# One accumulation for both heads of a pair, v in whole float32 beside zeros

## The chip, the core and the metric

The kernel runs on one core of a Trainium2 chip. The metric is the device time of one launch in microseconds: 1524.37 us, the median of three runs (1522.56, 1524.37 and 1529.31 us). TensorE is called PE below, its weight loads PEld; VectorE is DVE, ScalarE is ACT, GpSimd is POOL, SyncE is SP, which issues most DMAs.

## What is computed

Attention over 4 batches of 12 heads (448 positions, 64 values per head) with normalised q and k, followed by two mixers in float32, the first of rank 32 over the tokens and with 24 chunks of 128 channels, the second with a token mix and 12 chunks.

```python
q_n, k_n = rmsnorm(q, g_q), rmsnorm(k, g_k)
scores = np.matmul(q_n, k_n.transpose(0, 1, 3, 2)) / np.sqrt(64)
attn = softmax(scores)                       # with + 1e-9 below the line
x = np.matmul(attn, v)                       # (4, 12, 448, 64), then (4, 448, 768)
u = x + ((x.T @ U) @ V).T                    # first mixer
x = u + np.maximum(u @ w_ch1, 0) @ w_ch2     # w_ch1: 768 x 3072
h = np.maximum(x.T @ w_tok1, 0) @ w_tok2     # second mixer
u = x + h.T
out = u + np.maximum(u @ w_ch1b, 0) @ w_ch2b # 768 x 1536
```

The inputs of the mixers are float64, and the kernel turns their bits into float32 itself.

## The kernel before

Matmuls run in two forms: whole float32 operands (F32), or operands cut into a high and a low part of type float32r (F32R), whose products are added up. `split` (line 148) cuts: ACT writes the high part, POOL subtracts it for the low one.

The heads are taken in pairs, which share a tile of 128 partitions (2 x 64) of the result xT. The 12 pairs of batches 0 and 1 run alone: this is the lone stage. After it PE does the rank mix (`rank_mix`, line 588) of both batches, and the 12 pairs of batches 2 and 3 are woven into the channel mixer of the first two (`run`, line 1027). `attention` (line 513) sets the steps: at each step the softmax of a head two ahead, the weighting of the present one, the loads of a pair seven and five steps ahead. The program text is only the first order: a scheduler with a timeline model orders the instructions of each engine by readiness and by the buffers of the pools, so a change in one engine's load moves instructions on all of them. Engines then work in that order.

Per head the lone stage makes four score tiles sc (`softmax`, line 450): two F32R matmuls each, a maximum on DVE, the exponential on ACT, the scaling of p on POOL. `weigh` (line 471) then goes through four chunks of 112 keys: PE transposes four pieces of p into a PSUM tile pt, which is copied to SBUF as ph, and PE multiplies v by ph into the PSUM tile pv. The head of a pair with j = 0 is whole: v goes in as loaded (vr) and ph is a plain copy, by ACT or DVE in turn. The weights are 128 columns, of which the first 64 are the chunk's v, and only the first 64 rows of pv are used. The head with j = 1 is cut: v is split into vs (lines 403 to 410), ph is rounded to F32R by ACT, DVE makes the low part pl (line 502), and each chunk takes two F32R matmuls, of vs by ph and by pl. Its weights hold the high part of v beside the low one, so the two halves of pv are added at the end: ACT copies one to tmp (line 510), DVE adds it (line 511). For j = 0, DVE copies the half (line 507). In the woven stage both heads are cut.

In the lone stage the PSUM pools have 3 banks for sc ("s"), 1 for tt ("t"), and 4 ("p") that pt and pv share. In the trace one whole product of 448 columns shows as two MATMUL records, and one F32R product as one.

The mixer's weights are loaded in chunks (`load_w`, line 154): a DMA into w_raw, `to_f32` (line 118: ACT lines 130 and 135, DVE lines 131, 132 and 136, POOL line 139), then `split`. Their buffers hold two chunks of raw words and four of split weights.

Of the kernel before, what the change touches and what calls it, by code (L numbers as in the profile page):

```python
# [9 lines left out]
F32 = mybir.dt.float32  # L10
# [14 lines left out]
def attention_then_two_mixers(  # L25
# [30 lines left out]
    nc = tc.nc  # L56
    P = 128
    B, H, S, D = q.shape
# [298 lines left out]
    def fetch_heads(b, hp, names):  # L357

        h0 = 2 * hp
        res = []  # L360
        for nm in names:
            t = pools["at"].tile([CP, 2, NC4, D], F32, tag="vr" if nm == "v" else "qkr", bufs=AT[nm + "r"],
                        name=f"{nm}r")
            nc.sync.dma_start(t, dict(q=q, k=k, v=v)[nm][b, h0:h0 + 2].rearrange(
                "h (p c) d -> p h c d", c=NC4))
            res.append(t)
        return res

    def load_pair(b, hp, turn, qk):
        first = turn == 0  # L370
        mul = nc.vector.tensor_mul if turn in (0, 2, 3) else nc.gpsimd.tensor_mul
        qr, kr, vr = qk + fetch_heads(b, hp, "v")
# [30 lines left out]
    def split_v(vr, whole):  # L403
        vs = pools["at"].tile([CP, 2, NC4, 2, D], F32R, tag="vs", bufs=AT["vs"], name="vs")
        js = [j for j in range(2) if j not in whole]
        if js:
            js = slice(js[0], js[-1] + 1)
            split(vr[:, js], vs[:, js, :, 0], vs[:, js, :, 1])
        flat = vr.rearrange("p h c d -> p (h c d)")
        return [flat[:, j * NC4 * D:] if j in whole else vs[:, j] for j in range(2)]  # L410
# [59 lines left out]

    def weigh(pr, vj, j, dst, whole):

        pv = psum("v", [P, S], "pv")

        def product(kc, ph, pl):
            if whole:
                mm(pv, vj[:, kc * D:kc * D + P], ph, kc == 0, kc == NC4 - 1)
                return
# [27 lines left out]
        if whole:  # L506
            nc.vector.tensor_copy(dst[j * D:(j + 1) * D], pv[:D])
            return
# [4 lines left out]
    def attention(pairs, seam):  # L513
# [13 lines left out]
        for t in range(-8, n):  # L527
# [5 lines left out]
            if t >= 0:  # L533
                if t % 2 == 0:
                    dst = pairs[t // 2][3]()
                steps.append(weigh(
                    probs.pop(t), values[t // 2][t % 2], t % 2, dst, t % 2 in pairs[t // 2][2]))
# [19 lines left out]
            if 0 <= h < n:  # L557
                loaded[h // 2] = load_pair(
                    *pairs[h // 2][:2], h // 2, fetched.pop(h // 2))
# [499 lines left out]
    with ExitStack() as stack:  # L1059
# [3 lines left out]
        open_pools(inner, (("pp", 1, 0), ("s", 3, 1), ("t", 1, 1), ("p", 4, 1)))  # L1063
        pools["v"] = pools["p"]

        def new_xo():
# [3 lines left out]
            [(b, hp, (0,), lambda xT=xT, hp=hp: xT[:, hp], lambda dst: None)  # L1070
             for b, xT in zip((b0, b1), xs) for hp in range(NP)]
            + [(b, hp, (), new_xo,
                lambda dst, b=b, hp=hp: nc.sync.dma_start(xd[b][hp], dst))
               for b in (b2, b3) for hp in range(NP)], 2 * H)
# [114 lines left out]
```

## Time and profile before

| | us |
|---|---|
| median of three runs | 1524.37 |
| span of the profiled execution, first to last instruction | 1530.0 |
| lone stage, to the last addition into xT | 194.7 |
| rank mix of both batches and first products of the mixer | 194.7 to 232 |
| PE / DVE / POOL / ACT busy over the span | 1440.5 / 1177.0 / 908.4 / 745.0 |
| PE weight loads busy | 1274.2 |

The page gives no time for the profiled execution besides its span, which is 5.6 us over the median of the timed runs. Busy times are the union of an engine's instructions; matmuls overlap in the records, so that the cost of one on PE is read from the distance between the starts of neighbours and not from its length.

### The profile page before, as it was taken

Reading aid. Unit: us, or ns where it says so; the run is one execution under the profiler, and the core shown is the slowest. Engines: PE = TensorE matmul, PEld = TensorE weight load, DVE = VectorE, ACT = ScalarE, POOL = GpSimd, SP = SyncE. Lnnn points to the kernel's source line nnn. Section 1 sums busy time; section 2 is a strip of 40 time slices with the busy share of each in tenths; the row PEclk is TensorE's granted clock in tenths of the full one; section 3 lists DMA queues with packets and bytes.
Section 4 is the critical chain, followed back from the end, with each engine's and each line's share of the span. In section 5 each row is a group of like instructions: output and inputs, shape, how many; then the busy total and the mean of one; then the engine's idle time right before and its main releaser. Section 6 shows DMA issues by size and latency. Waiting matters only on the chain.

```text
span 1530.0 us, 22086 instructions
## 1 busy us (share of the span) xinstructions
PE 1440.5 (94%) x7396; PEld 1274.2 (83%) x7396; DVE 1177.0 (77%) x1805; ACT 745.0 (49%) x1508; POOL 908.4 (59%) x943
## 2 busy tenths in 40 slices
PE   4899988999899999999999999999999999999998
PEld 3666767888788889888888998898999998988997
DVE  7898888977787788676757776477888988577786
ACT  4687765765565665444535343335343431334431
POOL 5889947777666565455655454037787855206842
PEclk9999989999999999999999999999999999999999
DMA  6676656866666565765637664354545363423433
GB/s 174 156 168 158 151 169 208 273 201 199 223 207 202 165 207 189 248 228 189 213 125 239 227 232 143 115 194 130 181 125 185 125 192 122 130 92 109 137 117 108
DMA packets 144385, 266.06 MB, mean 174 GB/s; under 512 B 12832, under 2 KB 104448, under 8 KB 144160
## 3 DMA queue, kind: packets, MB, share of 16 engines
q1 hardware_dynamic: 143952, 264.65, 55.4%
q8 instruction: 59, 0.97, 0.3%
q14 instruction: 54, 0.44, 0.1%
q10 hardware_dynamic: 320, 0.00, 0.0%
HBM read 149.72 MB, written 79.10 MB: 150 GB/s over the span
## 4 chain that ended last, share of the span: by engine, by line
PE 50%; DVE 9%; DMA 4%; ACT 3%; POOL 3%; issue 2%; SPq 0%; DVEq 0%; POOLq 0%; ACTq 0%
PE ps_x L79 23%; PE ps_p L79 10%; PE ps_g L79 10%; PE ps_t L79 2%; PE ps_u L79 2%; DVE w_bits L136 1%; DVE w_bits L131 1%; DVE w_bits L132 1%; PE pv L79 1%; ACT w_bits L130 1%; POOL w L150 1%; DMA w_raw<-in_moe_w_ch_dram 1%; PE pt L487 1%; DMA c_a<-w_bits 1%; DMA qs<-both 1%
## 5 line engine op out<-in xcount | busy, mean ns | idle before, releaser
L79 PE MATMUL ps_x<-gs,w 128*128 128x448 f32 x1440 | 326.2, 373 | 7.6 <-DVE gs L656 2.9
L79 PE MATMUL ps_g<-u,w 128*128 128x448 f32 x1440 | 313.3, 371 | 6.5 <-DVE u L583 2.6
L79 PEld LDWEIGHTS ps_x<-gs,w 128*128 128x128 f32 x1440 | 268.6, 191 | 33.7 <-DVE gs L656 5.8
L79 PEld LDWEIGHTS ps_g<-u,w 128*128 128x128 f32 x1440 | 270.5, 190 | 30.3 <-DVE u L583 3.5
L79 PE MATMUL ps_x<-gs,w_b 128*128 128x448 f32 x1026 | 228.7, 368 | 6.5 <-DVE xT L851 2.0
L139 POOL TENSOR_TENSOR w_bits<-w_bits,w_round 128x768 uint32<-128x768 uint32 (+3 forms) x80 | 145.0, 1812 | 119.9 <-DVE w_bits L136 68.3
L79 PEld LDWEIGHTS ps_x<-gs,w_b 128*128 128x128 f32 x1026 | 192.7, 189 | 24.7 <-DVE xT L851 3.4
L150 POOL TENSOR_TENSOR w<-w_bits,w 128x768 fp32r<-128x768 f32 (+3 forms) x82 | 148.1, 1815 | 83.0 <-ACT w L149 78.6
L686 DVE TENSOR_TENSOR xT<-ps_x,xT 128x448 f32<-128x448 f32 x216 | 132.3, 618 | 44.5 <-PE ps_x L79 42.1
L150 POOL TENSOR_TENSOR w_b<-w_f,w_b 128x384 fp32r<-128x384 f32 x104 | 118.8, 1155 | 61.5 <-ACT w_b L149 61.1
L79 PE MATMUL sc<-ks,qs 128*112 128x448 f32 x384 | 124.6, 410 | 20.1 <-ACT p L461 16.9
L468 POOL TENSOR_SCALAR p<-p,sm 112x448 f32<-112x448 f32 x192 | 131.2, 696 | 19.4 <-DVE sm L465 16.1
L300 POOL TENSOR_TENSOR w_f<-w_f 128x384 f32<-128x384 f32 x26 | 36.4, 1401 | 178.7 <-DVE pu L779 73.5
L461 ACT ACTIVATE p<-sc,nm 112x448 f32<-112x448 f32 x192 | 121.4, 635 | 39.1 <-DVE nm L459 37.6
L459 DVE TENSOR_REDUCE nm<-sc 112x1 f32<-112x448 f32 x192 | 116.1, 614 | 11.8 <-PE sc L79 11.3
L487 PEld LDWEIGHTS pt<-ident,p 112*112 112x112 f32 x768 | 89.6, 135 | 34.3 <-issue 12.7
L487 PE MATMUL pt<-ident,p 112*112 112x112 f32 x768 | 110.6, 262 | 4.8 <-DVE pl L502 3.7
L498 ACT ACTIVATE ph<-pt 112x448 fp32r<-112x448 f32 (+1 forms) x168 | 88.2, 544 | 38.9 <-PE pt L487 38.0
L131 DVE TENSOR_SCALAR w_bits<-w_bits 128x768 f32<-128x768 f32 (+3 forms) x80 | 66.7, 834 | 50.0 <-ACT w_bits L130 50.0
L135 ACT ACTIVATE w_round<-w_raw 128x768 uint32<-128x768 uint32 (+3 forms) x80 | 69.8, 873 | 66.9 <-POOL w_bits L139 62.4
L502 DVE TENSOR_TENSOR pl<-pt,ph 112x448 fp32r<-112x448 f32 x144 | 86.9, 615 | 19.2 <-ACT ph L498 18.7
L130 ACT ACTIVATE w_bits<-w_raw 128x768 f32<-128x768 f32 (+3 forms) x80 | 70.0, 875 | 58.7 <-POOL w L150 31.4
(141 smaller groups left out, 2724.1 us busy)
## 6 DMA issues: line engine op xcount, KB each, us to landing
w_raw<-in_moe_w_ch_dram SPq DMA_DIRECT2D x72, 768.0 KB, 5.2
w_b<-h_a SPq DMA_DIRECT2D x65, 384.0 KB, 4.2
h_a<-w SPq DMA_DIRECT2D x56, 384.0 KB, 2.7
ks<-both SPq DMA_DIRECT2D x92, 224.0 KB, 3.7
c_a<-w_bits SPq DMA_DIRECT2D x40, 384.0 KB, 4.8
w_f<-c_a SPq DMA_DIRECT2D x40, 384.0 KB, 3.1
h_b<-w SPq DMA_DIRECT2D x32, 384.0 KB, 2.5
w_b<-h_b SPq DMA_DIRECT2D x29, 384.0 KB, 3.9
```

The source lines that it names most:

```text
L79: nc.tensor.matmul(o, lhsT=l, rhs=r, start=start, stop=stop)
L130: nc.scalar.activation(f(w), f(high), AF.Abs)
L131: nc.vector.tensor_scalar_max(f(w), f(w), TINY)
L139: nc.gpsimd.tensor_tensor(w, w, r, op=ALU.add)
L150: nc.gpsimd.tensor_sub(lo, w, f(hi))
L459: nc.vector.tensor_reduce(nm, sc, axis=AX.X, op=ALU.max, negate=True)
L461: nc.scalar.activation(p, sc, AF.Exp, bias=nm, accum_out=sm[:, c % 2:c % 2 + 1])
L468: nc.gpsimd.tensor_scalar(x, x, sm[:, i:i + 1], 1.0, op0=ALU.mult, op1=ALU.mult)
L487: nc.tensor.transpose(pt[:, c * CP:(c + 1) * CP], pr[c][:, kc * CP:(kc + 1) * CP], ident[:CP, :CP],)
L498: nc.scalar.activation(ph, pt, AF.Copy)
L502: nc.vector.tensor_sub(pl, pt, f(ph))
L686: nc.vector.tensor_add(xT[:, dc], px, xT[:, dc])
```

## The change

In the lone stage both heads of a pair are whole. v is loaded into one of four fixed buffers of 112 x 4 x 3 x 64, whose middle third is set to zero once by POOL; the two heads go, by one DMA each, to the thirds beside it. The weights of j = 0 are then (v, 0) and those of j = 1 are (0, v), each 128 columns, and all eight products of the pair accumulate in one PSUM tile, with the first matmul of j = 0 as its start and the last of j = 1 as its end. One DVE copy of 128 x 448 takes it to xT. ph is a plain copy for both heads, two by ACT and two by DVE. The split of v, pl, tmp and the addition are gone from this stage. The four shared PSUM banks become three for pt ("p") and one for pv ("v"). The woven stage computes as before.

```diff
-    def fetch_heads(b, hp, names):
+    def fetch_heads(b, hp, names, padded=None):
...
         for nm in names:
-            t = pools["at"].tile([CP, 2, NC4, D], F32, tag="vr" if nm == "v" else "qkr", bufs=AT[nm + "r"],
-                        name=f"{nm}r")
-            nc.sync.dma_start(t, dict(q=q, k=k, v=v)[nm][b, h0:h0 + 2].rearrange(
-                "h (p c) d -> p h c d", c=NC4))
-            res.append(t)
+            src = dict(q=q, k=k, v=v)[nm][b, h0:h0 + 2].rearrange("h (p c) d -> p h c d", c=NC4)
+            if nm == "v" and padded:
+                w = padded.pop(0)
+                padded.append(w)
+                for j in range(2):
+                    nc.sync.dma_start(w[:, :, 2 * j], src[:, j])
+            else:
+                w = pools["at"].tile([CP, 2, NC4, D], F32, tag="vr" if nm == "v" else "qkr",
+                                     bufs=AT[nm + "r"], name=f"{nm}r")
+                nc.sync.dma_start(w, src)
+            res.append(w)
         return res
-    def load_pair(b, hp, turn, qk):
+    def load_pair(b, hp, turn, qk, padded):
         first = turn == 0
         mul = nc.vector.tensor_mul if turn in (0, 2, 3) else nc.gpsimd.tensor_mul
-        qr, kr, vr = qk + fetch_heads(b, hp, "v")
+        qr, kr, vr = qk + fetch_heads(b, hp, "v", padded)
...
     def split_v(vr, whole):
+        if whole:
+            return [vr[:, :, j:j + 2].rearrange("p c h d -> p c (h d)") for j in range(2)]
         vs = pools["at"].tile([CP, 2, NC4, 2, D], F32R, tag="vs", bufs=AT["vs"], name="vs")
-        js = [j for j in range(2) if j not in whole]
-        if js:
-            js = slice(js[0], js[-1] + 1)
-            split(vr[:, js], vs[:, js, :, 0], vs[:, js, :, 1])
-        flat = vr.rearrange("p h c d -> p (h c d)")
-        return [flat[:, j * NC4 * D:] if j in whole else vs[:, j] for j in range(2)]
+        split(vr, vs[:, :, :, 0], vs[:, :, :, 1])
+        return [vs[:, j] for j in range(2)]
...
+    joint = []
+
     def weigh(pr, vj, j, dst, whole):
-        pv = psum("v", [P, S], "pv")
+        pv = joint.pop() if whole and j else psum("v", [P, S], "pv")
+        if whole and not j:
+            joint.append(pv)
...
             if whole:
-                mm(pv, vj[:, kc * D:kc * D + P], ph, kc == 0, kc == NC4 - 1)
+                mm(pv, vj[:, kc], ph, j == 0 and kc == 0, j == 1 and kc == NC4 - 1)
                 return
...
         if whole:
-            nc.vector.tensor_copy(dst[j * D:(j + 1) * D], pv[:D])
+            if j:
+                nc.vector.tensor_copy(dst, pv)
             return
...
-    def attention(pairs, seam):
+    def attention(pairs, seam, padded):
...
                 steps.append(weigh(
-                    probs.pop(t), values[t // 2][t % 2], t % 2, dst, t % 2 in pairs[t // 2][2]))
+                    probs.pop(t), values[t // 2][t % 2], t % 2, dst, pairs[t // 2][2]))
             for _ in zip_longest(*steps):
...
                 loaded[h // 2] = load_pair(
-                    *pairs[h // 2][:2], h // 2, fetched.pop(h // 2))
+                    *pairs[h // 2][:2], h // 2, fetched.pop(h // 2), h < seam and padded)
                 if h == 0:
...
         AT.update(p=12, ph=4, pl=4)
-        open_pools(inner, (("pp", 1, 0), ("s", 3, 1), ("t", 1, 1), ("p", 4, 1)))
-        pools["v"] = pools["p"]
+        open_pools(inner, (("pp", 1, 0), ("s", 3, 1), ("t", 1, 1), ("p", 3, 1), ("v", 1, 1)))
+        padded = []
+        for i in range(4):
+            padded.append(pools["pp"].tile([CP, NC4, 3, D], F32, tag=f"vp{i}", name="vr"))
+            nc.gpsimd.memset(padded[i][:, :, 1], 0.0)
...
         att = attention(
-            [(b, hp, (0,), lambda xT=xT, hp=hp: xT[:, hp], lambda dst: None)
+            [(b, hp, True, lambda xT=xT, hp=hp: xT[:, hp], lambda dst: None)
              for b, xT in zip((b0, b1), xs) for hp in range(NP)]
-            + [(b, hp, (), new_xo,
+            + [(b, hp, False, new_xo,
                 lambda dst, b=b, hp=hp: nc.sync.dma_start(xd[b][hp], dst))
-               for b in (b2, b3) for hp in range(NP)], 2 * H)
+               for b in (b2, b3) for hp in range(NP)], 2 * H, padded)
...
```

The scheduler's order of the whole lone stage and of the woven stage is another with the change; behind the last attention step the orders of all engines agree. Two places matter below. The first is PE in the middle of the lone stage. Before, the products of one pair's cut head (vs) and of the next pair's whole head (vr) alternate, in two PSUM tiles:

```order
L79 MATMUL pv<-pl,vs 128x448
L79 MATMUL pv<-ph,vs 128x448
L487 MATMUL pt<-ident,p 112x112 x4
L79 MATMUL sc<-ks,qs 112x448 x2
L79 MATMUL pv<-ph,vr 128x448
L79 MATMUL sc<-ks,qs 112x448 x2
L79 MATMUL pv<-pl,vs 128x448
L487 MATMUL pt<-ident,p 112x112 x4
L418 MATMUL tt<-ident,qn 128x112 x4
L79 MATMUL pv<-ph,vr 128x448
L487 MATMUL pt<-ident,p 112x112 x4
```

With the change, the end of the fourth pair and the start of the fifth; all eight products of a pair go into the one tile, and the second vr row below is the fourth pair's last:

```order
L79 MATMUL pv<-ph,vr 128x448
L495 MATMUL pt<-ident,p 112x112 x4
L79 MATMUL sc<-ks,qs 112x448 x6
L79 MATMUL pv<-ph,vr 128x448
L495 MATMUL pt<-ident,p 112x112 x8
L422 MATMUL tt<-ident,qn 128x112 x4
L495 MATMUL pt<-ident,p 112x112 x2
L79 MATMUL sc<-ks,qs 112x448 x2
L495 MATMUL pt<-ident,p 112x112
L79 MATMUL sc<-ks,qs 112x448 x2
L495 MATMUL pt<-ident,p 112x112
L79 MATMUL pv<-ph,vr 128x448 x3
```

The pairs no longer overlap in their products: 12 transposes pt, 4 transposes tt and 4 score matmuls stand between the last product of one pair and the first of the next. Over the eleven seams of the stage there stand 8 to 16 pt there, with up to 8 sc and at most 4 tt.

The second place is DVE, where it first meets a chunk of the mixer's weights (w_bits of 128 x 768). Before, that is behind the last addition into xT, among the rank mix's work (xs):

```order
L502 TENSOR_TENSOR pl<-pt,ph 112x448
L379 TENSOR_REDUCE ms<-sq 112x8
L511 TENSOR_TENSOR xT<-pv,tmp 64x448
L577 TENSOR_TENSOR xs<-pt_x,xs 112x384 x2
L131 TENSOR_SCALAR w_bits<-w_bits 128x768
L132 TENSOR_SCALAR w_bits<-w_bits 128x768
L136 SCALAR_TENSOR_TENSOR w_bits<-w_raw,w_bits 128x768
L577 TENSOR_TENSOR xs<-pt_x,xs 112x384 x2
```

With the change, that is in the middle of the lone stage, around the fifth of its twelve copies into xT:

```order
L504 COPY ph<-pt 112x448
L463 TENSOR_REDUCE nm<-sc 112x1 x3
L131 TENSOR_SCALAR w_bits<-w_bits 128x768
L516 COPY xT<-pv 128x448
L385 TENSOR_REDUCE ms<-sq 112x8
L504 COPY ph<-pt 112x448
L132 TENSOR_SCALAR w_bits<-w_bits 128x768
L463 TENSOR_REDUCE nm<-sc 112x1 x2
L136 SCALAR_TENSOR_TENSOR w_bits<-w_raw,w_bits 128x768
L469 RECIPROCAL sm<-sm 112x2
```

By the end of the lone stage DVE and POOL have converted none of these chunks before, and four with the change; ACT and POOL have also split two of the four there.

## Rows read from the trace of the kernel before

**Rows 1.** Windows: us, busy (instructions) of PE, PEld, DVE, ACT, POOL, clock, DMA, GB/s.

```profile
0.00:45.00 45.00, 24.62 (x111) 17.56 (x112) 33.50 (x64) 21.03 (x58) 25.94 (x55) 0.92 0.70 177
45.00:175.00 130.00, 119.11 (x682) 88.34 (x681) 114.28 (x238) 100.02 (x274) 116.64 (x213) 0.99 0.64 158
175.00:194.70 19.70, 16.63 (x96) 11.59 (x94) 14.90 (x29) 13.03 (x32) 16.87 (x34) 0.97 0.64 169
194.70:232.00 37.30, 31.95 (x147) 25.67 (x148) 32.18 (x55) 24.61 (x45) 15.22 (x11) 0.88 0.51 172
232.00:620.00 388.00, 368.00 (x1978) 326.64 (x1977) 311.64 (x526) 236.40 (x487) 258.28 (x284) 0.98 0.66 206
```

**Rows 2.** Groups of PE, 45 to 175 us: count, busy, mean ns, idle before.

```profile
L79 PE MATMUL sc<-ks,qs 128*112 128x448 f32 x152 | 49.6, 416 | 6.5 <-ACT p L461 5.0 <-DMA ks<-both 1.5
...
L487 PE MATMUL pt<-ident,p 112*112 112x112 f32 x300 | 40.4, 259 | 0.5 <-DVE sm L465 0.3 <-ACT ph L498 0.2
L79 PE MATMUL pv<-ph,vr 112*128 112x448 f32 x75 | 35.5, 554 | 0.0
...
L79 PE MATMUL pv<-ph,vs 112*128 112x448 f32 x37 | 16.8, 453 | 0.4 <-ACT ph L498 0.3
...
L418 PE MATMUL tt<-ident,kn 112*128 112x112 f32 x40 | 5.9, 272 | 0.0
```

**Rows 3.** Timeline of PE: start, length over the merged instructions, both us.

```profile
106.75 0.37 PE L79 MATMUL pv<-pl,vs 112*128 112x448 f32 x1
106.95 0.55 PE L487 MATMUL pt<-ident,p 112*112 112x112 f32 x4
...
107.74 0.92 PE L79 MATMUL pv<-ph,vr 112*128 112x448 f32 x2
108.50 0.55 PE L487 MATMUL pt<-ident,p 112*112 112x112 f32 x4
108.88 0.93 PE L79 MATMUL pv<-ph,vr 112*128 112x448 f32 x2
```

**Rows 4.** Waits of PE, 45 to 175 us: total us, times, longest.

```profile
PE sc L79 <- ACT p L461: 5.0, 8, 2.3
```

**Rows 5.** Groups of DVE, ACT, POOL for v, 45 to 175 us.

```profile
L502 DVE TENSOR_TENSOR pl<-pt,ph 112x448 fp32r<-112x448 f32 x38 | 22.8, 612 | 2.2 <-ACT ph L498 2.1
...
L498 ACT ACTIVATE ph<-pt 112x448 fp32r<-112x448 f32 x37 | 19.4, 548 | 5.3 <-PE pt L487 5.1
...
L496 DVE COPY ph<-pt 112x448 f32<-112x448 f32 x19 | 11.7, 615 | 0.1
...
L150 POOL TENSOR_TENSOR vs<-vr,vs 112x256 fp32r<-112x256 f32 x9 | 6.6, 728 | 0.1
...
L511 DVE TENSOR_TENSOR xT<-pv,tmp 64x448 f32<-64x448 f32 x9 | 5.6, 618 | 0.7 <-ACT tmp L510 0.4
...
L510 ACT ACTIVATE tmp<-pv 64x448 f32<-64x448 f32 x10 | 5.4, 541 | 0.2
...
L149 ACT ACTIVATE vs<-vr 112x256 fp32r<-112x256 f32 x10 | 4.2, 416 | 4.9 <-PE pv L79 4.9
```

**Rows 6.** Timeline around one copy of a weighted sum.

```profile
178.20 0.92 PE L79 MATMUL pv<-ph,vr 112*128 112x448 f32 x2
...
180.47 0.61 DVE L507 COPY xT<-pv 64x448 f32<-64x448 f32 x1
```

**Rows 7.** Groups of DVE for the weights, 192 to 232 us.

```profile
L136 DVE SCALAR_TENSOR_TENSOR w_bits<-w_raw,w_bits 128x768 uint32<-128x768 uint32 x4 | 4.4, 1092 | 0.0
...
L131 DVE TENSOR_SCALAR w_bits<-w_bits 128x768 f32<-128x768 f32 x4 | 2.2, 560 | 0.7 <-ACT w_bits L130 0.6
L132 DVE TENSOR_SCALAR w_bits<-w_bits 128x768 uint32<-128x768 uint32 x4 | 2.2, 553 | 0.0
```

**Rows 8.** Groups of POOL for the weights, 192 to 232 us.

```profile
L150 POOL TENSOR_TENSOR w<-w_bits,w 128x768 fp32r<-128x768 f32 x4 | 7.5, 1884 | 3.9 <-ACT w L149 3.9
L139 POOL TENSOR_TENSOR w_bits<-w_bits,w_round 128x768 uint32<-128x768 uint32 x4 | 7.5, 1865 | 18.2 <-DVE w_bits L136 18.2
```

## Prediction

> **What bounds the kernel now.** The first view is the windows by stage. The reader is to see that four engines are dense in the lone stage: from 45 to 175 us PE is busy 119.1 of 130 us, POOL 116.6, DVE 114.3, ACT 100.0 [rows 1]. No engine alone is full, and each could be the one that sets the pace. PE's busy share is flattering, because matmuls overlap in the records, so I count what PE has to do from the distances between starts. In the timeline of PE an F32R product is followed after 0.20 us (106.75 to 106.95), four transposes after 0.38 us (108.50 to 108.88, 0.095 each), and a whole float32 product, which has two records, after 0.76 us (107.74 to 108.50) [rows 3]. The groups give the counts: 152 sc at 0.20 are 30.4 us, 300 pt at 0.095 are 28.5, 75 records of vr, so 37.5 products at 0.76, are 28.5, the 37 products with ph and vs and as many with pl are 15 together at 0.20, and 80 tt (40 of k shown, 40 of q) are 7.6 [rows 2]. The sum is 110.0 us of 130, 85%. 37.5 products are 9.4 pairs: 13.8 us per pair, 11.7 of them work of PE. The waits say what the other 20 us are: small gaps, the largest group 5.0 us of sc for the exponential on ACT [rows 4]. So the lone stage is a chain through four nearly full engines, with PE at 85%.
>
> The next stretch is another case. From 194.7 to 232 us PE is busy 31.9 of 37.3 us at a mean clock of 0.88, and DVE 32.2, while POOL has only 15.2 [rows 1]. There the rank mix needs DVE for short steps, and DVE converts four chunks of weights between them [rows 7]; POOL waits 18.2 us for these conversions [rows 8].
>
> **What the change costs on PE.** Per pair four chunks of the cut head go from two F32R products (0.40) to one whole product (0.76): 4 x 0.36 = 1.44 us more, 17.3 us over 12 pairs. I take the same 0.76 for weights with zeros, since the columns streamed are the same 448. In the 9.4 pairs of the middle stretch it is 13.5 us: 123.5 us of work.
>
> **What it takes off the others.** Per pair DVE loses four pl (0.612) and the addition (0.618), gains two copies ph (0.615), and has one copy into xT as before, of 128 rows instead of 64 (both ends of the row count I price at 0.61): 1.84 us less, 22 us in all. ACT loses two ph (0.548), tmp (0.541) and the high part of v (0.416): 2.05 us, 25 in all. POOL loses the low part of v, 0.73 us, 9 in all [rows 5, 6]. None of this is a gain by itself. What it buys is that PE waits less, at most the 20 us that PE has free.
>
> **What the lone stage makes of it.** If PE were never idle, 123.5 us would be left of the 130; if PE stayed idle as long as now, 143.5. Between these I need PE's share in a stretch where the other engines are less full. The nearest is the woven stage: 1978 matmuls in 388 us [rows 1], of which 480 are transposes by the code (24 heads by 16 and 12 pairs by 8); 480 x 0.095 + 1498 x 0.20 = 345 us is 89%, an estimate, since some have fewer columns. There DVE is at 80% and POOL at 67%; with the change DVE would be at about 75% here (114.3 less 9.4 x 1.84), POOL still over 80%. I take 91%: 123.5 / 0.91 = 135.7, +5.7 us. Bounds: 96% gives -1.4, the idle time of now +13.5. The other 2.6 pairs stand at the ends of the stage, where PE is less dense (24.6 of 45 us, 16.6 of 19.7 [rows 1]); of their 3.7 us on PE I count half, 1.8, and the last head loses pl and tmp from its chain (0.61 + 0.54): +0.6 together. The lone stage: +6.3 us, between -2 and +17.
>
> **The conversions that move.** The order puts the conversion of four weight chunks into the lone stage, where DVE now has room. In the stretch from 192 to 232 us four of them cost DVE 4 x (0.560 + 0.553 + 1.092) = 8.8 us [rows 7]. They lie on the engine that is 86% busy there and that PE waits for, so I count most of it, -7 us; the bounds are -8.8 (all of it) and 0 (PE's lower clock and the chain of the rank mix bind alone). In the lone stage they are paid in DVE's free time, and POOL takes four additions of 1.87 and two subtractions of 1.88 us more, 11 us against the 9 that it loses [rows 5, 8]: POOL stays as full as it was. This is why I don't go above 91% for PE.
>
> **At nothing.** Four memsets of 112 x 256: a POOL subtraction of that size takes 0.73 us [rows 5], so at most 2.9 us at the start, where POOL is idle 19 of 45 us [rows 1]; if this cover failed, +2.9. Twelve more v loads on SP: they are issued five steps ahead into four fixed buffers, and a buffer comes free three heads before. The woven stage has another order but the same instructions, 0 with 3 us either way.
>
> **The one PSUM tile for pv.** The first product of a pair now waits until DVE has copied the pair before. In the trace a whole pair of records began at 178.20 and ended at 179.12, the copy began at 180.47 and ended at 181.08: 2.0 us behind the product [rows 6]. What hides it is the work of PE between two pairs in the new order. At the costs of [rows 3] the eleven seams have 1.1 to 3.1 us, mostly 2.3, so only the last one shows, 0.8 us, which lies within my bounds. On this the Trainium skill (Perfetto Trace Analysis, Matmuls) speaks against the change: independent groups of matmuls should rotate through different PSUM banks, so that the evacuation of one overlaps the next. By that rule the seam is a rival, below.
>
> **Sum.** +6.3 - 7 = -0.7 us on the profiled span of 1530.0, which is 5.6 us over the median; on the median of 1524.4 it gives 1523.7.
>
> **Rivals.** First, PE was not the limit, and fills up once DVE and ACT have room: 96% in the lone stage (-1.4) and all of the conversions (-8.8), 1514.2. For it: the largest wait of PE [rows 4] is for ACT, which is relieved. Against it: POOL is not relieved, and PE's free share would have to fall from 15 to 4%. The Trainium skill (Perfetto Trace Analysis, Identifying the Most-Contended Engine) would favour this one: it takes the busy share of the weight loads, not of the matmuls, as the measure of how full TensorE is. That share is 88.3 of 130 us, 68%, and both forms of product load two sets of weights, so by it nothing becomes tighter. But the starts in the timeline differ, 0.76 against 0.40 us, and this the weight loads don't show.
>
> Second, the gaps of PE are the latency of the chain and not the load of other engines, so that they stay: +17.3 - 7 = +10.3, 1534.7. For it: the gaps are many and short, and the products now come in blocks. Against it: DVE alone gets back 1.84 of 13.8 us per pair.
>
> Third, slower by the one PSUM tile: the copy stands in DVE's queue behind maxima, sums and a conversion of weights, and PE, which works in order, holds everything behind the first product, the scores too, so that DVE gets its next work late. It decides from 2.3 us between the last product and the end of the copy. At 3.0 us the eleven seams lose 7 us, at 3.5 us 12; with the latter 6.3 + 12 - 7 = +11, 1535.7. Against it: 2.0 us in the trace, with a fuller DVE.
>
> **How the numbers follow.** The forecast gets 0.50, the first rival 0.25, the second 0.15, the third 0.10. 1512 to 1536 leaves out the ends where both terms fall on one side; the forecast's own range is 1517 to 1531. Half a percent, 7.6 us, is about what can be told from no change. Faster by more: most of the first rival and a little of the forecast, 0.25; slower: most of the last two, 0.22; within: 0.53.
>
> **What would show it.** Starts of whole products 0.76 us apart from what follows them; a lone stage that ends near 201 us, with some 14.3 us per pair in the middle and PE waiting for POOL and ACT in small pieces; the first products of the mixer with hardly a conversion of DVE before them, and the point that was reached at 232 us reached some 30 us after the end of the lone stage. A wait of PE for L516, the copy into xT, of more than 0.5 us per pair would be the third rival. I am wrong if the lone stage ends before 194 or after 206 us, or if the stretch behind it takes as long as before.

## The result, and the profile after

The changed kernel takes 1547.18 us against 1526.84 us of the kernel before on the same chip, a ratio of 1.0149 (95% interval 1.0109 to 1.0189): slower by some 20 us, where 1523.7 us and a range of 1512 to 1536 were forecast. Timed again beside the experiments it was 1543.92 against 1521.32 us, 1.0138 (1.0108 to 1.0169).

The windows of the changed kernel (columns as in [rows 1]) are cut at the end of its lone stage (212.7 us), at the first product ps_x of the channel mixer (243.3) and at the 145th (369.6):

```profile
45.00:175.00 130.00, 118.54 (x600) 79.17 (x600) 97.81 (x197) 83.21 (x226) 112.68 (x187) 0.97 0.76 188
175.00:212.70 37.70, 35.42 (x186) 23.50 (x184) 23.95 (x49) 19.41 (x50) 30.37 (x61) 1.00 0.45 112
212.70:243.30 30.60, 25.48 (x135) 21.56 (x136) 21.65 (x43) 14.18 (x31) 1.84 (x1) 0.96 0.04 14
243.30:369.60 126.30, 112.12 (x590) 97.59 (x588) 99.81 (x170) 76.41 (x161) 94.16 (x107) 0.96 0.71 213
```

The same cuts of the kernel before, at 194.7, 229.3 and 345.5 us, and the stretch behind them up to its 289th ps_x:

```profile
194.70:229.30 34.60, 29.32 (x137) 23.68 (x137) 29.48 (x51) 21.91 (x41) 12.71 (x9) 0.87 0.47 155
229.30:345.50 116.20, 108.16 (x569) 92.80 (x568) 98.72 (x164) 73.42 (x154) 86.20 (x99) 0.99 0.74 228
345.50:449.40 103.90, 95.43 (x509) 85.59 (x507) 81.71 (x136) 60.78 (x127) 71.70 (x82) 0.95 0.64 196
```

The lone stage is 18.0 us longer, the stretch to the first ps_x 4.0 us shorter, and the next 144 products take 10.1 us more. In the windows from 45 to 175 us DVE fell from 114.3 to 97.8 of 130 us and ACT from 100.0 to 83.2, while POOL went from 116.6 to 112.7 and the DMA share rose from 0.64 to 0.76. The last row belongs to the profiled execution of before alone: it spent 103.9 us there at a clock of 0.95, and a variant with the same number of products in this stretch takes 96.8 us at 1.00 (below). So traces are compared up to 345 us only, and totals by the timed runs.

The groups of PE in the changed kernel, 45 to 175 us, answer to [rows 2]:

```profile
L79 PE MATMUL pv<-ph,vr 112*128 112x448 f32 x130 | 59.5, 557 | 0.7 <-ACT ph L506 0.7
L79 PE MATMUL sc<-ks,qs 128*112 128x448 f32 x139 | 44.0, 412 | 6.2 <-ACT p L465 5.9
L495 PE MATMUL pt<-ident,p 112*112 112x112 f32 x263 | 39.8, 267 | 4.6 <-ACT ph L506 2.8 <-POOL p L472 1.1 <-DVE ph L504 0.7
L422 PE MATMUL tt<-ident,kn 112*128 112x112 f32 x36 | 5.5, 274 | 0.0
L422 PE MATMUL tt<-ident,qn 112*128 112x112 f32 x32 | 4.4, 259 | 0.0
```

By the distances of [rows 3] this is 65 x 0.76 + 139 x 0.20 + 263 x 0.095 + 68 x 0.095 = 108.7 us of work in 130, 84%, where it was 85%. 65 products are 8.1 pairs, 16.0 us each. The distances themselves hold; in the timeline of PE a whole product starts, and what follows it 0.75 us later:

```profile
94.37 0.91 PE L79 MATMUL pv<-ph,vr 112*128 112x448 f32 x2
95.12 0.93 PE L495 MATMUL pt<-ident,p 112*112 112x112 f32 x8
```

The waits of PE from 45 to 212.7 us (total, times, longest) are small pieces as in [rows 4], and the copy out of the joint tile is waited for once:

```profile
PE sc L79 <- ACT p L465: 5.9, 6, 2.4
PE pt L495 <- ACT ph L506: 2.8, 2, 1.8
PE pv L79 <- DVE xT L516: 1.3, 1, 1.3
```

### The profile page after: what moved, and what is told of

The parts are those of the page before. It is cut to its first block, busy times and chain, and to the rows that moved or that the text cites. A ratio compares the mean times of both kernels' runs of the same rounds, so it can differ in the third digit from the quotient of the medians.

```text
span 1542.2 us, 22000 instructions
## 1 busy us (share of the span) xinstructions
PE 1450.7 (94%) x7396; PEld 1268.2 (82%) x7396; DVE 1157.3 (75%) x1769; ACT 723.1 (47%) x1460; POOL 905.7 (59%) x935
## 4 chain that ended last, share of the span: by engine, by line
PE 44%; DVE 6%; DMA 3%; POOL 3%; ACT 2%; issue 2%; SPq 0%; POOLq 0%; ACTq 0%; DVEq 0%
PE ps_x L79 21%; PE ps_p L79 10%; PE ps_g L79 8%; PE ps_u L79 2%; PE ps_t L79 2%; POOL w L150 1%; DVE w_bits L131 1%; POOL w_bits L139 1%; DMA c_a<-w_bits 1%; ACT w_bits L130 1%; DVE w_bits L136 1%; DVE w_bits L132 1%; DMA w_raw<-in_moe_w_ch_dram 1%; ACT w L149 1%; PE pt_x L579 1%
## 5 line engine op out<-in xcount | busy, mean ns | idle before, releaser
L472 POOL TENSOR_SCALAR p<-p,sm 112x448 f32<-112x448 f32 x192 | 139.7, 740 | 23.3 <-DVE sm L469 21.0
L495 PE MATMUL pt<-ident,p 112*112 112x112 f32 x768 | 113.9, 264 | 6.5 <-POOL p L472 2.8
L131 DVE TENSOR_SCALAR w_bits<-w_bits 128x768 f32<-128x768 f32 (+3 forms) x80 | 70.2, 877 | 59.3 <-ACT w_bits L130 59.2
L79 PE MATMUL ps_p<-t,w_b 128*128 128x448 f32 x432 | 95.1, 366 | 0.1
L799 ACT ACTIVATE pu<-pu 128x448 f32<-128x448 f32 x56 | 32.4, 579 | 132.5 <-DVE pu L788 132.1
```

The source lines that it names most:

```text
L79: nc.tensor.matmul(o, lhsT=l, rhs=r, start=start, stop=stop)
L131: nc.vector.tensor_scalar_max(f(w), f(w), TINY)
L472: nc.gpsimd.tensor_scalar(x, x, sm[:, i:i + 1], 1.0, op0=ALU.mult, op1=ALU.mult)
L495: nc.tensor.transpose(pt[:, c * CP:(c + 1) * CP], pr[c][:, kc * CP:(kc + 1) * CP], ident[:CP, :CP],)
```

## Experiments on the two parts

Ends of the lone stage are the ends of the last write into xT in the timeline of DVE; before it is 194.7 us. Ratios are to the kernel before, with 95% intervals.

**hold** keeps the conversions behind the lone stage, by marks on its last copy, ph and p:

```diff
...
-        w1s = [w1_chunk("a", wa1, j) for j in range(G)]
+        with behind("lone"), behind("lone_act"), behind("lone_pool"):
+            w1s = [w1_chunk("a", wa1, j) for j in range(G)]
```

> The changed kernel with the conversions of the mixer's first two weight chunks queued behind the lone stage on DVE, ACT and POOL, as they stood in the kernel before. Theory PE: the 17 us of added product time pace the stage, so its end stays near 210 us and the total within 1542 to 1552. Theory weights: the conversions, with ACT waiting for their DMA, hold the in-order engines up in the middle of the stage; then its end falls to about 203 us and the total to some 1533 to 1538.

Measured: lone stage to 207.5 us, 1535.56 us, ratio 1.0093 (1.0061 to 1.0125). Its windows, cut at the same points and with the stretch to the 289th ps_x:

```profile
45.00:175.00 130.00, 121.30 (x632) 82.55 (x631) 93.05 (x196) 77.78 (x221) 106.67 (x204) 0.98 0.65 155
...
207.50:242.80 35.30, 29.03 (x135) 23.92 (x135) 29.11 (x52) 20.08 (x38) 11.80 (x7) 0.85 0.44 145
242.80:358.70 115.90, 107.94 (x569) 92.79 (x568) 94.39 (x165) 73.18 (x154) 87.85 (x99) 0.99 0.74 230
358.70:455.50 96.80, 92.00 (x509) 81.95 (x507) 80.52 (x135) 60.59 (x127) 72.26 (x82) 1.00 0.68 209
```

The end lies near that of the theory of PE, the total in the range of the theory of the weights: each has a part. From 207.5 us on the stretches take as long as in the kernel before, up to the one in which the trace of the kernel before has the lower clock; what is left are 12.8 us in the lone stage.

**half** leaves the conversions and cuts the second head's four products to half the columns, so that PE has as much to do per pair as before:

```diff
-                mm(pv, vj[:, kc], ph, j == 0 and kc == 0, j == 1 and kc == NC4 - 1)
+                n = S // 2 if j else S
+                mm(pv[:, :n], vj[:, kc], ph[:, :n], j == 0 and kc == 0, j == 1 and kc == NC4 - 1)
```

> The changed kernel, with the four products of the second head of a pair cut to 224 of 448 columns (half of that head's result is left out), so that PE's work per pair is 4 x 0.76 + 4 x 0.38 = 4.6 us, as in the kernel before, and all else is as with the change. Theory PE: the end of the lone stage falls to 194 to 198 us, the total to 1525 to 1532. Theory weights: at least half of the 18 us stay, the stage ends at 203 us or later, the total is over 1536.

Measured: lone stage to 207.4 us, ratio 1.0043 (1.0014 to 1.0071). The end speaks for the theory of the weights, the total of 1529.6 us for that of PE: of 12.7 us more in the lone stage the timed runs keep 6, and where the rest is given back is not traced. Nor are the 12.7 us all work and waits: from 45 us to the end of the stage the mean granted clock was 0.93, in the kernel before and in hold 0.98. At two levels of 2.4 and 1.2 GHz that is worth at most 0.05 x 162 = 8 us, by estimate.

**hold_half** has both edits.

> The changed kernel with both suspected causes taken out: the second head's four products cover 224 of 448 columns (its half of the sum is incomplete by that), and the weight conversions stay behind the lone stage. PE's work per pair is then that of the kernel before. Theory of two causes (added product time of about 17 us, and conversions inside the lone stage): the lone stage ends within 4 us of 194.7, ratio 0.995 to 1.003. Rival, that the joint tile, the blocks of products or the padded v cost something by themselves: the lone stage ends 6 to 12 us late as in the runs with only one cause removed (+12.7 and +12.9), ratio 1.004 or more.

Measured: lone stage to 194.4 us, ratio 1.0023 (1.0000 to 1.0046). So the two parts are the loss but for 3.5 us (0.0023), whose interval reaches zero; the joint tile, the padded v and the new order cost nothing in the lone stage that the relief of DVE and ACT does not cover.

**oldwhole** makes both heads whole in the kernel before, without padded v and joint tile: each head has its own pv, and the weights are 128 neighbouring columns of v.

```diff
...
-            [(b, hp, (0,), lambda xT=xT, hp=hp: xT[:, hp], lambda dst: None)
+            [(b, hp, (0, 1), lambda xT=xT, hp=hp: xT[:, hp], lambda dst: None)
...
```

> The kernel before with both heads whole in its old layout: one v tile, one DMA, a PSUM tile and a DVE copy for each head, the four shared banks. PE has the same added 17 us; the order leaves the weights' conversions at the stage's end. Theory PE: total 1540 to 1550, the stage ends near 210 us. Theory weights: 1528 to 1535. If the one PSUM tile or the two v DMAs cost something of their own, this one is faster than the changed kernel by that.

Measured: lone stage to 209.1 us, ratio 1.0113 (1.0080 to 1.0145). The longer products alone, in the old layout, cost about what they cost in hold, 14.4 us against 12.8, though the first conversion stands in the last 6 us of this stage.

**early** is the kernel before with only the conversions moved into the lone stage (`w1s = ...` at step t = 10 instead of behind the last).

> The kernel before with the loads of the first two weight chunks issued at the step of the tenth head, so that their conversions fall into the lone stage, nothing else changed. Theory PE: the total stays at 1523 to 1531. Theory weights: the stage ends 5 us later or more, and the total is 1533 to 1542 unless the stretch behind it gets shorter by as much, as the prediction took it (7 us).

Measured: lone stage to 208.8 us, ratio 1.0103 (1.0071 to 1.0134). The conversions alone cost as much as the products alone (early's mean clock over the same stretch was 0.96), and both together 18.0 us, not 28: the two overlap. So how the 18.0 is divided depends on which is taken out first. By hold it is 12.8 for the products and 5.2 for the conversions on top of them, by half 12.7 for the conversions and 5.3 for the products.

## Experiments on what sets the pace

**both_cut** is the opposite of the change: `(0,)` of the kernel before becomes `()`, and both heads take F32R products.

> The kernel before with both heads of a lone pair cut, the opposite step to the change: per pair PE loses 1.44 us (17 over the stage), DVE gains some 1.8, ACT 2.1, POOL 0.7 us (22, 25, 9). Theory that PE and DVE are equally tight in the kernel before, so that work added to either shows in full and work taken from one shows nothing: the lone stage ends 12 to 25 us late, ratio 1.006 to 1.016. Rival, that PE alone is the bound there: it ends 8 us early or more, ratio 0.996 or less.

Measured: lone stage to 220.7 us, a microsecond behind the expected range, ratio 1.0157 (1.0132 to 1.0182). PE alone was not the bound. But DVE, ACT and POOL all got work here, and the mean clock from 45 us to the end was 0.92 (before 0.98), worth at most 0.06 x 176 = 11 of the 26.0 us by the same estimate; the run does not tell these apart. The next one adds work to DVE alone.

**sq_before** gives DVE the squares of all lone pairs in the kernel before:

```diff
-            mul(sq, tt, tt)
+            (nc.vector.tensor_mul if turn < 12 else mul)(sq, tt, tt)
```

> The kernel before, the squares of q and k of all lone pairs on DVE: POOL 18.7 us less over the stage, DVE some 13 us more. Theory that POOL at 90% sets the pace of the lone stage before the change: it ends 5 to 12 us earlier than 194.7, ratio 0.992 to 0.997. Rival, that PE's small gaps are latency or that DVE at 88% is as full: within 3 us or later, ratio 0.998 to 1.004.

Measured: lone stage to 207.5 us, ratio 1.0155 (1.0124 to 1.0186). The theory on POOL fell: POOL went down to 103.1 of 130 us, and the 13 us that DVE got came out as 12.8 us, at a clock of 0.97. (The timed runs lose 21.7 us; behind the stage the stretch to the first ps_x took 41.3 us at a clock of 0.75, where the kernel before has 34.6 at 0.87.) In the middle of the stage DVE is busy 112 to 115 of 130 us in before, early, both_cut and sq_before alike, whatever is added, which fits an engine without more room. PE's wait for the exponential, which stands behind DVE's maximum, rose from 5.0 us [rows 4] to

```profile
PE sc L79 <- ACT p L461: 12.1, 15, 1.6
```

**sq_hold** and **sq_hold_half** do the same to hold and to hold_half.

> The changed kernel with the conversions held behind the lone stage, and the squares of all lone pairs on DVE, which has 93 of 130 us there. Theory that the longer products make PE the bound of this stage (121 of 130 us): it ends within 3 us of the run that only holds the conversions (207.6), ratio 1.006 to 1.010. Rival, that POOL still sets the pace: it ends 6 us earlier or more, ratio 1.005 or less.

> The changed kernel with the conversions held and the second head's products on 224 columns (the run that came out as the kernel before, lone stage 194.4 us), and the squares of all lone pairs on DVE: 13 us more for DVE, 18.7 less for POOL, as in the run that did this to the kernel before and made its lone stage 12.8 us longer. Theory that DVE is tight before and has room with the change: the lone stage ends within 4 us of 194.4. Rival, that the squares on DVE cost by their place in the order, whatever DVE's load: 9 us later or more.

Measured: 210.1 us against 207.5 (ratio 1.0091, 1.0064 to 1.0117), and 199.6 us against 194.4 (1.0058, 1.0036 to 1.0081). In the first the theory of PE held. With 22 us less on DVE the same 13 us cost 3 to 5 instead of 13. The second was expected within 4 us, and lies just outside.

**hold_quarter** takes PE further down: of a pair's eight products only the first has all columns (`n = S // 2 if j or kc else S`).

> The changed kernel, conversions held behind the lone stage, and of the eight products of a pair only the first covers all 448 columns, the other seven 224 (so both heads' sums are incomplete). Products of a pair: 0.76 + 7 x 0.38 = 3.42 us against 4.64 before and 4.56 with only the second head cut: 1.14 us per pair and 14 us over the stage less for PE, nothing else changed on the other engines. Theory that with the DVE, ACT and POOL work of the changed kernel PE alone sets the pace: the lone stage ends 8 to 14 us before 194.7, ratio 0.990 to 0.996. Rival, that the chain through the other engines sets it at this point: it ends within 3 us of 194.7, ratio 0.998 to 1.003.

Measured: lone stage to 194.1 us, ratio 1.0028 (1.0010 to 1.0046): the rival. PE lost 14 us of work and waited longer, most for the copies of k:

```profile
PE sc L79 <- DMA ks<-both: 8.5, 6, 2.6
```

The same count of PE's work as above, from 45 to 175 us of each (a product of 224 columns at 0.38, the distance in that timeline). The prices are those of the full clock; the mean clock was 0.93 in both_cut and 0.95 to 0.99 in the others, so that both_cut's share is too low:

| | pv records | sc, pt, tt | work of 130 us | lone stage ends |
|---|---|---|---|---|
| before | 75 vr, 74 vs | 152, 300, 80 | 110.0, 85% | 194.7 |
| both_cut | 134 vs | 136, 264, 74 | 86.1, 66% | 220.7 |
| sq_before | 70 vr, 67 vs | 140, 277, 72 | 101.1, 78% | 207.5 |
| hold_quarter | 144 vr | 153, 294, 76 | 96.5, 74% | 194.1 |
| hold_half | 152 vr | 158, 307, 76 | 111.3, 86% | 194.4 |
| hold | 138 vr | 142, 280, 72 | 114.3, 88% | 207.5 |
| after | 130 vr | 139, 263, 68 | 108.7, 84% | 212.7 |

From the kernel before, work added to PE or to DVE lengthens the stage by about three quarters of it or more. Work taken from DVE (hold_half) or from both (hold_quarter) shortens nothing: these two end within 0.6 us of the kernel before. What holds them at 194 us is not shown; both ran at a clock of 0.95 to 0.96 in the middle of the stage (before 0.99), which hides at most some 5 us.

## Experiments on the conversions

**sq_early** tried POOL as the price of the moved conversions, with early's conversions and the squares on DVE.

> The kernel before with the conversions moved into the lone stage, as in the run that did this alone, but the squares of q and k of all lone pairs on DVE: nine pairs by two by 1.04 us = 18.7 us less for POOL. Theory that the moved conversions cost because POOL, 117 of 130 us busy in the middle of that stage, takes 11 us more: the lone stage ends less than 6 us after 194.7 instead of 14.1. Rival, that ACT and DVE stand in order behind conversions that wait for their words from memory: it still ends 10 us late or more. DVE gets about 13 us more, so a loss through a full DVE (it had 112 of 130 us) would also show as 10 us or more, with PE's waits naming DVE.

Measured: lone stage to 226.6 us, ratio 1.0207 (1.0182 to 1.0233). POOL at 103.9 us did not help; the 13 us of DVE came on top, as 17.8 us against early. This says that DVE, at 113.3 us, is full, and nothing on the conversions.

**words** lets the first two chunks be converted from a small tile loaded at the start.

> The changed kernel, but the first two of the four weight chunks converted inside the lone stage read a small tile that lies in the chip from the start, in place of the words that their DMA brings (the DMAs remain; the weights are wrong by it); the other two find free buffers for their words early. The engines' work is as in the changed kernel, the waits of ACT and DVE for the words (4.2 and 3.8 us) should be gone. Theory that these waits, handed on in order, are what the moved conversions cost in the lone stage: it ends within 2 us of the run that holds the conversions back (207.5). Rival, that the work itself costs: it ends at 211 us or later, as the changed kernel (212.7).

Measured: lone stage to 212.6 us, ratio 1.0102 (1.0075 to 1.0129). Inconclusive: ACT still waited 4.2 us for words, those of the next chunks.

**after_again** and **hold_again** time the two kernels side by side.

> The changed kernel again, timed beside the one that holds the conversions back. Theory that the conversions inside the lone stage cost something of their own: 0.3 to 0.8% more than that run, ratio about 1.015. Rival, that they only move time about: the two agree within 0.2%.

> The changed kernel with the conversions held behind the lone stage, again, beside the changed kernel: ratio about 1.009 by the theory of two causes (1.007 to 1.011); the same as the changed kernel, 1.013 or more, if the first comparison was chance.

Measured: 1.0138 (1.0108 to 1.0169) and 1.0075 (1.0052 to 1.0098); 1543.92 - 1535.33 = 8.6 us between them, of which the lone stage has 5.3 (213.1 against 207.8).

**words4** converts all four chunks from the small tile:

```diff
...
+        fixed = pools["fixed"].pop() if pools["fixed"] else None
+        if fixed is not None:
+            words = fixed.bitcast(U32).rearrange("p (n t) -> p n t", t=2)
+            low, high = [words[:, :, i].unsqueeze(1).to_broadcast([P, 32, DM // 32]) for i in range(2)]
...
```

> The changed kernel, all four weight chunks of the lone stage converted from a small tile that lies in the chip from the start (the DMAs of the words remain; the weights are wrong by it). ACT's wait for words in that stage should be gone, which is to be seen in the waits. Theory that these waits are the price: the lone stage ends at 205 to 209 us instead of 212.7, as with the conversions held back. Rival, that the price is the work (ACT some 2.7, DVE 2.2, POOL 3.7 us per chunk): it ends at 211 us or later.

Measured: lone stage to 217.4 us, ratio 1.0192 (1.0165 to 1.0218). A fifth chunk had moved up, and ACT stood 5.8 us for its words: inconclusive again. By the copies into xT the changed kernel and hold go side by side up to 126 us, one of the four conversions in (the changed kernel is 2.0 us ahead), and part in one pair; the timeline of DVE in the changed kernel, and then in hold:

```profile
125.79 0.62 DVE L516 COPY xT<-pv 128x448 f32<-128x448 f32 x1
...
147.70 0.61 DVE L516 COPY xT<-pv 128x448 f32<-128x448 f32 x1
...
212.08 0.63 DVE L516 COPY xT<-pv 128x448 f32<-128x448 f32 x1 [1.65 <-PE pv L79]
```

```profile
127.76 0.60 DVE L517 COPY xT<-pv 128x448 f32<-128x448 f32 x1
...
141.16 0.61 DVE L517 COPY xT<-pv 128x448 f32<-128x448 f32 x1
...
206.92 0.62 DVE L517 COPY xT<-pv 128x448 f32<-128x448 f32 x1 [1.65 <-PE pv L79]
```

21.9 us for that pair against 13.4. In these 20 us the words are loaded. The windows of the changed kernel, then of hold; the last two columns are the DMA share and GB/s:

```profile
120.00:130.00 10.00, 9.96 (x54) 6.48 (x53) 8.12 (x17) 6.80 (x20) 9.51 (x14) 1.00 0.69 163
130.00:140.00 10.00, 9.17 (x51) 6.14 (x49) 5.33 (x12) 5.26 (x15) 9.24 (x21) 1.00 1.00 293
140.00:150.00 10.00, 7.02 (x32) 5.12 (x31) 9.28 (x13) 5.22 (x11) 7.98 (x10) 0.83 0.97 197
```

```profile
120.00:130.00 10.00, 9.37 (x53) 6.56 (x54) 8.32 (x19) 6.92 (x20) 7.05 (x16) 1.00 0.78 185
130.00:140.00 10.00, 10.00 (x52) 6.78 (x51) 5.97 (x12) 6.08 (x17) 8.68 (x18) 1.00 0.35 80
140.00:150.00 10.00, 9.43 (x53) 6.51 (x51) 5.23 (x13) 3.92 (x11) 7.01 (x16) 1.00 0.77 180
```

The DMA engines are full for 20 us, and the lone stage needs them: qs and ks are copied by DMA on their way to PE. In the changed kernel itself two loads of words are issued from 131.3 us on and land 8 and 11 us later; ACT stands for both, with exponentials and copies ph behind it, and PE for these (timeline of the changed kernel, all engines):

```profile
131.29 1.53 SPq L121 DMA_DIRECT2D w_raw<-in_moe_w_ch_dram  x2
...
139.73 0.92 ACT L130 ACTIVATE w_bits<-w_raw 128x768 f32<-128x768 f32 x1 [2.73 <-DMA w_raw<-in_moe_w_ch_dram]
...
142.10 0.66 PE L79 MATMUL sc<-ks,qs 128*112 128x448 f32 x2 [1.18 <-ACT p L465]
...
143.56 0.91 ACT L130 ACTIVATE w_bits<-w_raw 128x768 f32<-128x768 f32 x1 [1.51 <-DMA w_raw<-in_moe_w_ch_dram]
...
144.95 1.20 PE L495 MATMUL pt<-ident,p 112*112 112x112 f32 x6 [1.80 <-ACT ph L506]
```

That left two causes, the wait for the words and the copies that queue beside them. **words_held** is words4 with the fifth and sixth chunk behind the lone stage; **no_words** also leaves out the four DMAs:

```diff
...
-        for o, d in srcs(raw):
+        for o, d in srcs(raw) if not pools["fixed"] else ():
...
```

> The changed kernel, the four weight chunks of the lone stage converted from a small tile that is there from the start (wrong weights by it), and the fifth and sixth chunk held behind the lone stage, so that nothing in it waits for words, while the DMAs of the four chunks and the work of four conversions remain. Theory that the waits for words, handed on in order, are what the moved conversions cost in the stage: it ends at 204 to 209 us, as without conversions (207.5). Rival, that the work of ACT, DVE and POOL for them costs: 211 us or later.

> The same without the DMAs of the four chunks (3.1 MB less to load by then). If the waits for words alone are the price: within 2 us of the run that keeps these DMAs. Rival, that the DMAs delay the loads of q, k and their copies, for which ACT waits in the stage: the lone stage ends 4 us or more before that run's.

Measured: lone stage to 215.1 us (ratio 1.0212, 1.0187 to 1.0237) and to 205.7 us (1.0131, 1.0098 to 1.0164). The theory that the waits for words alone are the price fell: without any, the stage ends later than in the changed kernel. The rival on the DMAs held: without the four loads it ends 9.4 us earlier. With the loads and no wait for words the pair at 120 us takes 25.3 us, without them 19.8. What ACT waits for, 45 to 205 us, are the copies, in words_held and then in no_words:

```profile
ACT both L441 <- DMA qs<-both: 18.6, 6, 7.1
```

```profile
ACT both L441 <- DMA qs<-both: 4.4, 1, 4.4
```

The time from issue to landing of qs, 120 to 165 us (min, median, max), in the order changed kernel, hold, words_held, no_words:

```profile
DMA to landing us min/median/max: 3.2/5.0/11.1
```

```profile
DMA to landing us min/median/max: 2.1/2.2/5.1
```

```profile
DMA to landing us min/median/max: 2.1/3.9/9.0
```

```profile
DMA to landing us min/median/max: 2.1/2.5/4.0
```

So, as far as these traces go, the loads are the larger part, and they work in two ways: the words come late (the changed kernel), or the copies of q and k do (words_held), for which ACT waits before it may overwrite `both`; DVE and PE stand behind ACT, each in its order. They are not the whole. That no_words ends 1.8 us before hold is no proof that the work of the conversions is free, for it was 4.9 us ahead at the sixth copy into xT, and takes 19.8 us for the pair where hold takes 13.4:

```profile
122.91 0.61 DVE L529 COPY xT<-pv 128x448 f32<-128x448 f32 x1
...
142.66 0.61 DVE L529 COPY xT<-pv 128x448 f32<-128x448 f32 x1
...
205.08 0.62 DVE L529 COPY xT<-pv 128x448 f32<-128x448 f32 x1 [1.65 <-PE pv L79]
```

From the sixth copy to the last, hold takes 79.2 us, no_words 82.2, the changed kernel 86.3 and words_held 94.3. Of the 7.1 us between hold and the changed kernel some 3 stay without the four loads, with the work of the conversions, the stores of what they split and two loads, of the fifth and sixth chunk, that no_words issues at 101 and 105 us. This split is from single traces whose orders differ.

## Why the prediction was wrong

**The work of PE was priced rightly**, 0.76 against 0.40 per chunk, and the savings nearly: in hold DVE does 19 us less than before over the lone stage, ACT 20 and POOL 7, where 22, 25 and 9 were counted.

**The step that failed first is PE's share.** "I take 91%: 123.5 / 0.91 = 135.7, +5.7 us" borrowed the woven stage's share for a stage in which other engines had been relieved. The share stayed at 84 to 88%, the second rival's case ("the gaps of PE are the latency of the chain"), with its +17.3 measured as +12.8 without the conversions. It had a chance of 0.15. (That the whole stage came out at +18.0 is luck for it: 5.2 of that is the conversions, which it left at nothing there.) The argument against it, "DVE alone gets back 1.84 of 13.8 us per pair", was the mistake: hold_half has these savings and PE's old work, and ends at 194.4 against 194.7; in hold_quarter PE is 74% full with DVE at 96 us, and the stage is not shorter either. Nor were 20 us of PE there to be bought: PE stood idle 10.9 of the 130 us [rows 1], and the rest of the 20 is the difference between the records and the distances. The reading that fits is that a pair's time is the longest path through PE, DVE, ACT and the copies by DMA, in their orders, and that room on one engine shortens it only where that engine is on the path; no run follows the path itself.

**The step that failed second is the conversions**: "In the lone stage they are paid in DVE's free time". They cost 5.2 us on top of the products, and 12.7 to 14.1 alone (half, early). A conversion also brings its load (128 x 768 words of 8 bytes, 0.79 MB a chunk), which the working left out; [rows 1] had the DMA share at 0.64 in that stage, and a stretch at 1.00 follows. And the free time is a mean: from 140 to 150 us, where the words land and two conversions come at once, DVE is busy 9.28 of 10. POOL, named as the engine at risk, is busier in no_words (118.2 of 130 us) than in the changed kernel (112.7), and no_words ends 7 us earlier, so its load is not the larger part of the price.

**Their return, "-7 us", came to -4.0**, and more was lost in the next stretch. Only four chunks fit in the buffers, so four made early mean that nothing is made between 212.7 and 243.3 us: the DMA moves 14 GB/s, and POOL does one thing,

```profile
L150 POOL TENSOR_TENSOR w<-w_bits,w 128x768 fp32r<-128x768 f32 x1 | 1.8, 1841 | 31.9 <-ACT w L149 31.9
```

At the first ps_x both kernels have four chunks converted on DVE, and the changed one resumes there. One subtraction on DVE then takes 3.38 us beside two POOL instructions of the resumed conversion, a maximum and an exponential stand behind it, and PE idles 3.89 us (timeline of the changed kernel, all engines); after_again shows the same, with 3.39 and 3.77:

```profile
248.62 1.81 POOL L139 TENSOR_TENSOR w_bits<-w_bits,w_round 128x768 uint32<-128x768 uint32 x1
249.30 3.38 DVE L592 TENSOR_TENSOR u<-xT,u 128x448 fp32r<-128x448 f32 x1
250.39 1.81 POOL L150 TENSOR_TENSOR w<-w_bits,w 128x768 fp32r<-128x768 f32 x1
...
254.03 1.09 PE L79 MATMUL sc<-ks,qs 128*112 128x448 f32 x2 [3.89 <-ACT p L465]
```

The clock fell with it: 0.84 and 0.77 in the first two 10 us of the stretch (before 0.93 and 0.90), and 0.96 against 0.99 over the whole, worth at most 4 us. PE idles once more, 3.6 us, at 342 us; the longest wait in this stretch of before is 1.4. And part of the 10.1 us is attention work that the new order puts there (590 matmul records against 569) and that the next stretch is spared (501 against 509). How the 10.1 us divide is not worked out. In the variants too the stretch is long where the clock is low: 115.9 us at 0.99 in hold, 134.8 at 0.90 in no_words, with 604 records.

**The joint tile** (third rival) cost 1.3 us, once, for the 0.8 us taken: right. The Trainium skill (Perfetto Trace Analysis, Matmuls) would have a second bank there; oldwhole, with a tile for each head in four banks, ends its lone stage at 209.1 us and hold, with the one tile, at 207.5, so nothing was to be had from it here. The first rival fell with DVE and ACT relieved and PE no fuller than 88%.

**The sum as it was**: +12.8 for the products and +5.2 for the conversions with their loads in the lone stage, -4.0 behind it, and +10.1 in the next stretch, for which the working had "0 with 3 us either way": 24.1 us at 369.6, of which the timed runs keep 20 to 23.

## What to carry to other kernels

Before a saving on one engine is counted as room for another, ask whether the stage is paced by a path through all of them: here added work showed by three quarters or more, and removed work didn't. A share of PE taken from another stage is no estimate for this one. The share of the stage itself, kept at 85%, gives 123.5 / 0.85 = 145.3, +15.3 us for the middle of the stage, against +12.8 measured for the whole: too much, but nearer than +6.3. Adding work to one engine at a time, as sq_before does, tells more than its share. Work that is moved takes its loads along, and they are priced against the DMA windows and the small copies of the stage that receives them. A producer that is already as far ahead as its buffers allow stands idle later by what it did earlier, 31 us here, and then resumes all at once.

## What the runs showed of the hardware

The same conversion on DVE takes longer in the lone stage, 2.98 us, than in [rows 7], where L131 took 560 ns, L132 553 and L136 1092, 2.21 us together; L136 alone does not. The groups of the changed kernel from 90 to 213 us:

```profile
L131 DVE TENSOR_SCALAR w_bits<-w_bits 128x768 f32<-128x768 f32 x4 | 4.9, 1232 | 3.4 <-ACT w_bits L130 3.4
L136 DVE SCALAR_TENSOR_TENSOR w_bits<-w_raw,w_bits 128x768 uint32<-128x768 uint32 x4 | 4.1, 1027 | 0.0
L132 DVE TENSOR_SCALAR w_bits<-w_bits 128x768 uint32<-128x768 uint32 x4 | 2.9, 716 | 0.1
```

They stand beside a POOL that is busy 87% of the time, in [rows 7] beside one at 41%; and POOL's scaling of p took 654 ns in the lone stage of before, 643 in hold, where no conversion of a chunk stands in the stage, and 714 with the change:

```profile
L472 POOL TENSOR_SCALAR p<-p,sm 112x448 f32<-112x448 f32 x60 | 42.1, 714 | 0.6
```

The Trainium skill (SBUF — State Buffer, SBUF: two separate sides) has a rule for this: VectorE, in an operation of a two-port mode or with two SBUF inputs, and GpSimd share a pair of ports by an exclusive lock, and the one that comes second waits. The trace agrees in sign (1232 against 560 ns), and in after_again it was 746 for the same line. It agrees in time too: the subtraction of 3.38 us above, which takes 0.61 us at 246.11, has two inputs in SBUF and ends 0.5 us behind the second of two POOL instructions that began before and during it. No run here sets the two engines against each other alone.
